# Attention on one core: block turns on VectorE, weighted sums on 32-row array tiles, scores as float32 products on 64-row tiles

## The chip, the cores and the metric

One core of a Trainium2 chip runs the kernel. The metric is device time in microseconds (us) of one execution; profiles give the times of single instructions on the five engines: TensorE (PE for its matmuls, PEld for its weight loads), VectorE (DVE), ScalarE (ACT), GpSimd (POOL) and SyncE (SP, which issues the DMAs).

## The reference

Attention over 8 batches, 8 heads, 576 positions and 64 dimensions, with a learned bias on the scores, and a feed-forward block behind it. All data is float32.

```python
scores = (q @ k.T) / 8                      # per batch and head, 576 x 576
x = log1p(abs(i - j)) / log1p(max(i, 1))    # relative position
bias = relu(x @ w1 + b1) @ w2               # one value per head, i, j
p = exp(scores + bias - rowmax)             # softmax over j
attn = p / (sum(p) + 1e-9)
y = attn @ v                                # -> 4608 tokens x 512
out = ((y @ moe_w1) * (y @ moe_w2)) @ moe_w3 @ moe_w_out
```

## The kernel before

**Stages.** First the bias of all heads is computed and written to DRAM (`nb_d`). Then comes the attention loop. Behind it `moe_w3 @ moe_w_out` is folded into one matrix (`fold`), and then the feed-forward block runs over nine chunks of 512 tokens (`up`, `down`).

**Units.** The loop runs over 32 units: four pairs of heads by eight batches. A unit has nine query tiles of 128 rows: four for each head of the pair (names 0 to 7, even ones of the first head) and a mixed tile M with the last 64 queries of both. In 24 units one piece of the feed-forward weights is also brought from its 64-bit input to float32 in eight small steps (`c0` to `c7`, made by `narrow`): a fetch, two on ScalarE, four on VectorE (clamp L132, shift L135, head L141, power L146) and a last one of two products on GpSimd (L149, L150).

**Steps of a unit.** GpSimd splits q and k into a rounded part and a rest (`op_g`, L250 to L257): the two parts of q stand one above the other on the 128 rows of a tile, k stands twice and its rest twice. `op_S` (L284) then makes a score tile from products of 288 columns over all 128 rows, two per half. `op_T` (L292) is one VectorE instruction that scales, adds the bias and keeps the row minimum of the negated scores; `op_E` (L315) is the exponential on ScalarE with the row sum; `op_r` (L322, L323) the reciprocal of the nine sums. `op_F` (L336 to L349) turns the 128x128 blocks of the exponentials on TensorE by a product with the identity, `op_H` (through `move`, L355 on VectorE and L357 on ScalarE) copies the turned blocks from PSUM to SBUF, and `op_W` (L391) makes the weighted sums from them, the two heads on the two column halves of the array, over 128 keys at a time; `op_X` copies the sums out, `op_x` stores them. The sums are divided later, in the feed-forward stage, by way of the reciprocals in `r_d` (L327, L328).

**Order.** Nothing is ordered by a scheduler: each step has an engine and a time relative to its unit's start in the table `ORDER`, units follow at `PERIOD`, and the steps are issued in the order of these times. An engine runs its instructions in that order and waits where data or a buffer is missing. `NPP`, `NTS` and `NPS` are numbers of buffers for exponentials, score passes and PSUM tiles; scores have two PSUM tiles.

Of the kernel before, what the change touches and what calls it, by code (L numbers as in the profile page):

```python
# [29 lines left out]
PERIOD = 15.82  # L30
ORDER = {
# [4 lines left out]
    },  # L36
    "DVE": {
        "T0": 0.98, "T1": 2.64, "T2": 3.63, "T3": 5.29, "T4": 6.16, "c3": 7.31, "c4": 8.31, "T6": 9.82, "T5": 10.52,
        "c5": 11.22, "c6": 12.22, "T7": 14.31, "H4": 15.01, "TM": 15.82, "HL0": 17.50, "r": 17.84, "HM": 20.14,
        "HN": 22.68,  # L40
    },
    "ACT": {
# [3 lines left out]
    },  # L46
    "POOL": {"gk": -15.50, "gq": -11.40},
    "SP": {"ldk": -30.00, "ldq": -28.00, "ldv": -10.00},
}
TILES = "01234567M"  # L50
NPP, NTS, NPS = 6, 3, 4


def arrange(NU, pieces):

    at = {n: (t, e) for e, steps in ORDER.items() for n, t in steps.items()}
    at["rd"] = at["HN"][0] + 0.8, "SP"
    at["xd"] = max(at["X0"][0], at["X1"][0]) + 0.8, "SP"
    at["c0"] = at["c1"][0] - 4.8, "SP"
    at["c7"] = max(at["c2"][0], at["c6"][0]) + 0.6, "POOL"  # L60
    return {(n, u): (u * PERIOD + t, e) for u in range(NU) for n, (t, e) in at.items() if n[0] != "c" or u in pieces}


@with_exitstack
def relpos_attention_moe(
# [42 lines left out]
    def narrow(pool, src, n, x, queue, pieces=1):  # L108
# [22 lines left out]
        def clamp():  # L131
            nc.vector.tensor_scalar(d["mag"], d["mag"], LEAST, MOST, op0=ALU.max, op1=ALU.min)  # L132
# [60 lines left out]
    st = {u: {"P": [None] * 9} for u in range(NU)}  # L193
# [3 lines left out]

    Q2 = []
    for i in range(2):
        qt = qk.tile([P, 2 * (S + P)], F32R, name=f"Q{i}")  # L200
        nc.gpsimd.memset(f(qt[:, S:S + P]), 0.0)
        Q2.append(qt)

# [7 lines left out]
    def load_bias(p, ts):  # L211
# [9 lines left out]
        if h == 0:  # L221
            nc.sync.dma_start(nb, rows)
        else:
            nc.sync.dma_start(nb[:, :, S - 512:S], rows[:, :, 0:512])
            nc.sync.dma_start(nb[:, :, 0:S - 512], rows[:, :, 512:S])
# [3 lines left out]
    def load(u, which):  # L229
        p, b = units[u]  # L230
        src = {"q": q, "k": k, "v": v}[which]
        if which == "v":
            t = vp.tile([P, v.shape[3]], F32, name="rv", bufs=3)
        else:
            t = raw.tile([P, 2 * S], F32, name=f"r{which}")
        nc.sync.dma_start(t, src[p, b])
        st[u]["r" + which] = t

    def op_ld(u, n):
        load(u, n[1])  # L240

    def op_g(u, n):

        d = st[u]
        x = d.pop("r" + n)
        if n == "q":
            Q = Q2[u % 2]
            Qd = halves(Q)[:, :, 0:S]
# [4 lines left out]
        else:
            K = qk.tile([P, 2 * S], F32R, name="K", bufs=2)
            kl = qk.tile([P, 2 * S], F32R, name="kl", bufs=2)
            nc.gpsimd.tensor_scalar(K, x, 1.0, 1.0, op0=ALU.mult, op1=ALU.mult)
            nc.gpsimd.tensor_tensor(kl, x, f(K), op=ALU.subtract)  # L257
            d.update(K=K, kl=kl)

    def op_S(u, t):  # L260
        d = st[u]
        Q, K, kl = d["Q"], d["K"], d["kl"]
        d["s", t] = ps_s.tile([P, 2, 512], F32, name="s")
        for hf in range(2):
            scores(d["s", t][:, hf, :HS], t, hf, Q, K, kl)

    def scores(s, t, hf, Q, K, kl):
        js = slice(hf * HS, (hf + 1) * HS)
        if t == "M":

            l, m = Q[:, 512:512 + P], Q[:, S + 64:S + 64 + P]
            ops = [(s, l, x[:, js]) for x in (K, kl)]
            if hf == 0:
                ops += [(s, m, x[:, S + 64:S + 64 + HS]) for x in (K, kl)]
            else:
                ops += [(s[:, 0:512 - HS], m, x[:, S + 64 + HS:2 * S]) for x in (K, kl)]
                ops += [(s[:, 512 - HS:HS], m, x[:, S:S + 64]) for x in (K, kl)]
# [509 lines left out]
```

## Time and profile before

| | before |
|---|---|
| median of 3 runs | 1251.35 us (1250.6 to 1251.85) |
| span of the profiled execution | 1248.1 us |
| TensorE matmuls busy | 1210.0 us, 97% |
| VectorE busy | 653.6 us, 52% |
| ScalarE busy | 603.1 us, 48% |
| GpSimd busy | 379.7 us, 30% |
| data moved by DMA | 130.26 MB, 104 GB/s |

The profiled execution is given by its span, from its first to its last instruction; the time of a run also holds what lies around that, and the median of the runs is 3.25 us above the span. In the rows of a profile `x16` is a count, a tile name left of the arrow is written, those right of it are read, `128*64` is the part of the array that is used (rows by columns) and `128x256` the shape of the output. A row in order of time begins with its start and its length in us; a bracket gives the idle time ahead of it and what ended it. A busy matmul is not a matmul at its peak: neighbours overlap, so their starts tell more than their lengths.

### The profile page before, as it was taken

The page shows a single profiled execution, that of the slowest core. Times are in us where ns is not written, and L with a number is a line of the kernel's source. Part 1 is how long each engine was busy: PE and PEld are TensorE (multiplying, and loading weights), DVE is VectorE, ACT ScalarE, POOL GpSimd, SP SyncE. Part 2 cuts the span into 40 slices and gives each one's busy share as a digit, 9 for nine tenths or more (in the row PEclk, how much of TensorE's full clock was granted, in tenths as well). Part 3 has the DMA queues.
Part 4 walks back from the last instruction along what each step waited for, and adds up shares of the span by engine and source line. Part 5 has one row for each costly group of instructions (what it writes and reads, how often), then busy time and mean ns, then how long its engine had stood idle before and what let it go on. Part 6 is the DMA issues. An engine that isn't in the chain of part 4 may idle for free.

```text
span 1248.1 us, 19110 instructions
## 1 busy us (share of the span) xinstructions
PE 1210.0 (97%) x7200; PEld 964.2 (77%) x7200; DVE 653.6 (52%) x1380; ACT 603.1 (48%) x1295; POOL 379.7 (30%) x256
## 2 busy tenths in 40 slices
PE   6789999999999999999999999999999999999998
PEld 1368887777777788887678888888888888888887
DVE  8957776777677767775797522222212231313111
ACT  3768887888788878888444221212121212121211
POOL 5026664666466655661444300000000000000000
PEclk9989999999999999999999999999999999999999
DMA  4874446444644564521543121211111120200000
GB/s 149 285 234 144 142 147 202 142 142 141 222 123 151 151 219 134 145 81 54 133 147 110 60 68 34 68 34 51 51 51 51 42 61 34 68 34 1 20 15 34
DMA packets 60220, 130.26 MB, mean 104 GB/s; under 512 B 8928, under 2 KB 17504, under 8 KB 60128
## 3 DMA queue, kind: packets, MB, share of 16 engines
q1 hardware_dynamic: 59696, 129.02, 33.1%
q8 instruction: 57, 0.93, 0.3%
q14 instruction: 35, 0.29, 0.1%
q10 hardware_dynamic: 432, 0.02, 0.0%
HBM read 99.10 MB, written 29.92 MB: 103 GB/s over the span
## 4 chain that ended last, share of the span: by engine, by line
PE 81%; DVE 10%; DMA 4%; ACT 3%; issue 2%; SPq 0%; ACTq 0%; POOL 0%; DVEq 0%; POOLq 0%
PE up L652 32%; PE o L677 16%; PE pst L391 13%; PE s L284 11%; PE pst L349 5%; DVE r L322 4%; DVE ts L292 3%; PE wacc L611 2%; DMA nb_d<-bev 2%; ACT pt L357 2%; PE bacc L511 1%; DVE zdve L497 1%; DVE px L355 1%; DVE r L323 0%; DMA wi<-in_moe_w_dram 0%
## 5 line engine op out<-in xcount | busy, mean ns | idle before, releaser
L292 DVE CUSTOM_DVE_ANT_0 ts<-s,nb 128x576 f32<-128x576 f32 x256 | 184.6, 748 | 134.7 <-ACT pt L357 73.7
L660 DVE TENSOR_TENSOR g<-up,a 128x512 f32<-128x512 f32 x72 | 49.7, 691 | 343.4 <-PE up L652 343.4
L652 PE MATMUL up<-xh,wl 128*128 128x512 f32 x576 | 225.1, 391 | 0.0
L652 PE MATMUL up<-xl,wh 128*128 128x512 f32 x576 | 225.1, 391 | 0.0
L652 PE MATMUL up<-xh,wh 128*128 128x512 f32 x576 | 225.1, 391 | 0.0
L315 ACT ACTIVATE pp<-ts,mx 128x576 f32<-128x576 f32 x256 | 196.6, 769 | 42.5 <-DVE mx L292 42.5
L284 PE MATMUL s<-K,Q 128*128 128x288 f32 (+2 forms) x672 | 205.6, 325 | 9.2 <-ACT bev L518 3.7
L284 PE MATMUL s<-kl,Q 128*128 128x288 f32 (+2 forms) x672 | 182.3, 295 | 0.0
L677 PE MATMUL o<-w3s,gh 128*128 128x512 f32 x576 | 177.7, 390 | 0.0
L657 ACT COPY a<-up 128x512 f32<-128x512 f32 x72 | 42.2, 587 | 259.6 <-PE up L652 259.6
L638 POOL TENSOR_SCALAR xh<-xr 128x512 fp32r<-128x512 f32 x36 | 23.2, 646 | 445.4 <-DVE xr L634 442.7
L349 PE MATMUL pst<-ident,pp 128*128 128x128 f32 x1024 | 152.4, 277 | 0.2 <-ACT pt L357 0.2
L284 PEld LDWEIGHTS s<-K,Q 128*128 128x128 f32 x672 | 128.0, 191 | 30.1 <-DVE mx L292 13.6
L357 ACT ACTIVATE pt<-pst 128x512 f32<-128x512 f32 x224 | 129.4, 593 | 29.1 <-PE pst L349 24.8
L391 PE MATMUL pst<-pt,rv 128*64 128x320 f32 (+1 forms) x1024 | 138.3, 412 | 1.4 <-DVE pt L355 1.4
L663 ACT ACTIVATE gh<-g 128x512 fp32r<-128x512 f32 x72 | 45.5, 633 | 178.3 <-DVE g L660 178.3
L349 PEld LDWEIGHTS pst<-ident,pp 128*128 128x128 f32 x1024 | 118.5, 141 | 15.7 <-DVE wi L146 11.8
L284 PEld LDWEIGHTS s<-kl,Q 128*128 128x128 f32 x672 | 129.0, 192 | 0.0
L652 PEld LDWEIGHTS up<-xh,wl 128*128 128x128 f32 x576 | 108.2, 188 | 23.4
L652 PEld LDWEIGHTS up<-xl,wh 128*128 128x128 f32 x576 | 108.2, 188 | 23.4
L652 PEld LDWEIGHTS up<-xh,wh 128*128 128x128 f32 x576 | 108.2, 188 | 23.4
L677 PEld LDWEIGHTS o<-w3s,gh 128*128 128x128 f32 x576 | 108.1, 188 | 22.9
(87 smaller groups left out, 1734.2 us busy)
## 6 DMA issues: line engine op xcount, KB each, us to landing
rk<-in_k_dram SPq DMA_DIRECT2D x32, 576.0 KB
rq<-in_q_dram SPq DMA_DIRECT2D x32, 576.0 KB
wi<-in_moe_w_dram SPq DMA_DIRECT2D x32, 512.0 KB
nb_d<-bev SPq DMA_DIRECT2D x36, 295.5 KB
rv<-in_v_dram SPq DMA_DIRECT2D x32, 320.0 KB
x_d<-x SPq DMA_DIRECT2D x32, 288.0 KB
xr<-x_d SPq DMA_DIRECT2D x36, 256.0 KB
rb<-r_d SPq DMA_DIRECT2D x72, 128.0 KB
```

The source lines that it names most:

```text
L284: nc.tensor.matmul(o, l, r, start=(m == 0), stop=(m == len(ops) - 1))
L292: nc.vector.tensor_tensor_reduce(out=halves(ts), in0=d.pop(("s", t))[:, :, :HS], in1=halves(NB[p, t]), op0=ALU.add, op1=ALU.min, scale=-1. ...
L315: nc.scalar.activation(pp, ts, AF.Exp, bias=mx, scale=-1.0, accum_out=d["sum"][:, col:col + 1])
L322: nc.vector.tensor_scalar(r, d["sum"], 1e-9, None, op0=ALU.add)
L349: nc.tensor.transpose(ps[:, c * P:(c + 1) * P], x, ident)
L357: nc.scalar.activation(o, x, AF.Copy)
L391: nc.tensor.matmul(acc[rows], x[:, c0:c0 + D], m, start=(c == 0), stop=(c == 4))
L652: nc.tensor.matmul(acc, l[:, cc], r, start=(n == 0), stop=(n == 3 * NC - 1))
L657: nc.scalar.copy(a, ps[0])
L660: nc.vector.tensor_tensor(g, ps[1], a, op=ALU.mult)
L663: nc.scalar.activation(gh, g, AF.Copy)
L677: nc.tensor.matmul(d["o", t], l[:, sl], folded[ft][:, r], start=(ft == 0 and n == 0), stop=(ft == NF - 1 and n == 2),)
```

## The change

Weighted sums no longer need a full turn. VectorE turns each exponential tile in blocks of 32x32 (`op_R`, into `PT`, SBUF to SBUF), so that a block's 32 keys lie on the 32 rows that its 32 queries had. `op_W` works on 32-row, 64-column tiles of the array: four row groups by two heads, eight tiles, for each of 18 blocks of 32 keys, in four parts (`PARTS`); each row group adds into its own PSUM bank (`acc`, one buffer of four banks). v is loaded four times, once for each row group. TensorE's turns, the copies of the turned blocks and the splitting of q and k on GpSimd go. Scores are plain float32 products on four tiles of 64x64: two halves of the keys on the two row halves, two groups of 64 queries on the two column halves. The reciprocals are turned on VectorE too, and their store takes twelve DMAs in place of two. The clamp of a weight piece moves from VectorE to GpSimd. q, k and v are laid out for this on the host, with no arithmetic. The table of times is replaced by a rule with one slot `L_T` per query tile.

```diff
+L_T = 1.39
+PERIOD = 9 * L_T
 TILES = "01234567M"
-NPP, NTS, NPS = 6, 3, 4
+NPP, NTS = 4, 3
+PARTS = ((0, 5), (5, 9), (9, 14), (14, 18))
+PART_AT = 12, 14, 16, 18
...
+    for k, t in enumerate(TILES):
+        a = k * L_T
+        at["S" + t] = a - 1.1, "PE"
+        at["T" + t] = a + 0.9, "DVE"
+        at["E" + t] = a + 1.7, "ACT"
+        at["R" + t] = a + 2 * L_T + 1.6, "DVE"
+    at["r"] = 10 * L_T + 1.55, "DVE"
+    at["rd"] = 10 * L_T + 2.5, "SP"
+    for n, k in enumerate(PART_AT):
+        at[f"W{n}"] = k * L_T - 0.6, "PE"
+    at["X"] = PART_AT[-1] * L_T + 1.5, "ACT"
+    at["xd"] = at["X"][0] + 0.8, "SP"
+    at["lk"] = -13.0, "SP"
+    at["lq"] = -12.9, "SP"
+    at["lv"] = 1.2 * L_T, "SP"
+    at["c0"] = 0.2, "SP"
+    at["c1"] = 5 * L_T + 2.5, "ACT"
+    at["c2"] = 6 * L_T + 2.5, "ACT"
+    at["c3"] = 6 * L_T + 2.0, "POOL"
+    for n in range(3):
+        at[f"c{4 + n}"] = (7 + n) * L_T + 2.0, "DVE"
+    at["c7"] = 9 * L_T + 3.0, "POOL"
...
-            nc.vector.tensor_scalar(d["mag"], d["mag"], LEAST, MOST, op0=ALU.max, op1=ALU.min)
+            nc.gpsimd.tensor_scalar(d["mag"], d["mag"], LEAST, MOST, op0=ALU.max, op1=ALU.min)
...
+    def op_l(u, which):
...
+            t = vp.tile([P, 2 * NBK * D], F32, name="v4")
+            for a in range(4):
+                nc.sync.dma_start(t[32 * a:32 * a + 32], v[p, b])
...
-    def op_g(u, n):
...
     def op_S(u, t):
+        s = d["s", t] = ps_s.tile([P, 2, 512], F32, name="s")
+        for hf, rows in enumerate((lo, hi)):
+            for g, outs in enumerate((lo, hi)):
...
+                nc.tensor.matmul(
+                    s[outs, hf, :HS], d["q"][rows, h * S + q0:h * S + q0 + 64],
+                    d["k"][rows, h * S + hf * HS:h * S + (hf + 1) * HS], start=True, stop=True,
+                )
...
+    def op_R(u, t):
+        nc.vector.transpose(PT[u % 2][:, SLOT[t]], st[u].pop(("p", t)))
...
+            r = SUMS[u % 3]
+            nc.vector.tensor_scalar(r[:, 0:9], r[:, 0:9], 1e-9, None, op0=ALU.add)
+            nc.vector.reciprocal(r[:, 0:9], r[:, 0:9])
+            d["rt"] = sm.tile([P, 32], F32, name="rt")
+            nc.vector.transpose(d["rt"], r)
...
+        for a in range(4):
+            for h in range(2):
+                o = rows[h, 0:512].rearrange("(i a j) -> a i j", a=4, j=32)[a]
+                nc.sync.dma_start(o, d["rt"][32 * a + 4 * h:32 * a + 4 * h + 4])
+            h, j = a // 2, 512 + a % 2 * 32
+            nc.sync.dma_start(rows[h:h + 1, j:j + 32], d["rt"][32 * a + 8:32 * a + 9])
...
-    def op_F(u, n):
...
-    def op_H(u, n, on):
...
     def op_W(u, n):
+        if n == "0":
+            d["acc"] = ps_t.tile([P, 4, 512], F32, name="acc")
+        acc, pt_, x = d["acc"], PT[u % 2], d["v"]
+        for b in range(*PARTS[int(n)]):
+            for a in range(4):
+                rows = slice(32 * a, 32 * a + 32)
+                for h, outs in enumerate((lo, hi)):
+                    t0, t1 = ((0, 5 if a < 2 else 4), (5 if a < 2 else 4, 9))[h]
+                    c0 = 0 if (h == 1 and a >= 2) else 32
+                    nc.tensor.matmul(
+                        acc[outs, a, c0:c0 + 32 * (t1 - t0)], x[rows, (h * NBK + b) * D:(h * NBK + b + 1) * D],
+                        pt_[rows, t0:t1, 32 * b:32 * b + 32], start=(b == 0), stop=(b == NBK - 1),
+                    )
+    def op_X(u, n):
...
+        nc.scalar.activation(
+            x[:, 0:512].rearrange("p (i a j) -> p a i j", a=4, j=32),
+            acc[:, :, 32:160].rearrange("p a (i j) -> p a i j", j=32), AF.Copy,
+        )
+        for outs, a0, c0 in ((lo, 0, 160), (hi, 2, 0)):
+            nc.scalar.activation(
+                x[outs, 512:S].rearrange("p (a j) -> p a j", j=32), acc[outs, a0:a0 + 2, c0:c0 + 32], AF.Copy,
             )
```

More of the change, by code (lines that the diff above doesn't have):

```diff
@@ L27 @@
 AT_W = 3.5, 0.0, 0.5, 1.2, 2.6, 3.8, 5.5, 7.1, 10.0, 10.6
-PERIOD = 15.82
-ORDER = {
[4 rows of a table removed]
[L36 to L42, printed above, removed]
[3 rows of a table removed]
[L46 to L49, printed above, removed]
+L_T = 1.39
+PERIOD = 9 * L_T
 TILES = "01234567M"
-NPP, NTS, NPS = 6, 3, 4
+NPP, NTS = 4, 3
+PARTS = ((0, 5), (5, 9), (9, 14), (14, 18))
+PART_AT = 12, 14, 16, 18
 def arrange(NU, pieces):
[L56 to L61, printed above, removed]
+    at = {}
+    for k, t in enumerate(TILES):
[20 more added lines that the diff above has]
+    at["c7"] = 9 * L_T + 3.0, "POOL"
+    return {(n, u): (u * PERIOD + t + 1.1, e) for u in range(NU) for n, (t, e) in at.items() if n[0] != "c" or u in pieces}
 @with_exitstack
@@ L192, in relpos_attention_moe @@
     NB = {}
[L193 to L202, printed above, removed]
+    st = {u: {} for u in range(NU)}
     def halves(x):
@@ L220, in load_bias @@
         rows = nb_v[2 * p + h, r0:r0 + 2 * P, :].rearrange("(k p) j -> p k j", p=P)
[L221 to L225, printed above, removed]
+        nc.sync.dma_start(nb, rows)
         for k, t in enumerate(ts):
             NB[p, t] = nb[:, k]
-    def load(u, which):
+    NBK = S // 32
+    def op_l(u, which):
         p, b = units[u]
-        src = {"q": q, "k": k, "v": v}[which]
@@ L260, in op_S @@
+            for a in range(4):
+                nc.sync.dma_start(t[32 * a:32 * a + 32], v[p, b])
+        else:
+            t = raw.tile([P, 2 * S], F32, name=which)
+            nc.sync.dma_start(t, {"q": q, "k": k}[which][p, b])
+        st[u][which] = t
     def op_S(u, t):
         d = st[u]
[L262 to L277, printed above, removed]
-        else:
-            h, i = int(t) % 2, int(t) // 2
-            q0 = h * (S + P + 64) + i * P
-            l = Q[:, q0:q0 + P]
-            ops = [(s, l, x[:, h * S + hf * HS:h * S + (hf + 1) * HS]) for x in (K, kl)]
-        for m, (o, l, r) in enumerate(ops):
-            nc.tensor.matmul(o, l, r, start=(m == 0), stop=(m == len(ops) - 1))
@@ L300, in op_T @@
             load_bias(p + 1, GROUP[t])
+    SUMS = []
+    for i in range(3):
+        t = att.enter_context(tc.tile_pool(name=f"sums{i}", bufs=1)).tile([P, 32], F32, name=f"sums{i}")
+        nc.gpsimd.memset(t, 1.0)
+        SUMS.append(t)
     def op_E(u, t):
@@ L378, in relpos_attention_moe @@
-    QS = (slice(0, 256), slice(256, S))
+            r = SUMS[u % 3]
[3 more added lines that the diff above has]
+            nc.vector.transpose(d["rt"], r)
+            return
+        rows = r_d[p][:, b * S:(b + 1) * S]
+        for a in range(4):
[4 more added lines that the diff above has]
+            nc.sync.dma_start(rows[h:h + 1, j:j + 32], d["rt"][32 * a + 8:32 * a + 9])
@@ L380, in op_W @@
     def op_W(u, n):
         d = st[u]
-        qs, x = QS[int(n)], d["rv"]
-        PT, PX = PTX[u % 2]
-        n_q = qs.stop - qs.start
-        acc = ps_t.tile([P, 512], F32, name="pst")[:, 0:n_q]
-        for c in range(5):
-            for h, rows in enumerate((lo, hi)):
-                c0 = (4 * h + c if c < 4 else 8 + h) * D
-                m = PT[:, c, h * S + qs.start:h * S + qs.stop] if c < 4 else PX[:, qs]
-                nc.tensor.matmul(acc[rows], x[:, c0:c0 + D], m, start=(c == 0), stop=(c == 4))
@@ L537, in relpos_attention_moe @@
     ps_s = att_r.enter_context(tc.tile_pool(name="ps_s", bufs=2, space=PSUM, side="right"))
-    ps_t = att.enter_context(tc.tile_pool(name="ps_t", bufs=NPS, space=PSUM))
-    PTX = [(pt.tile([P, 4, 2 * S], F32, name=f"pt{i}"), pt.tile([P, S], F32, name=f"px{i}")) for i in range(2)]
+    ps_t = att.enter_context(tc.tile_pool(name="ps_t", bufs=1, space=PSUM))
+    PT = [pt.tile([P, 9, S], F32, name=f"pt{i}") for i in range(2)]
     drive([e for e in later if e[0] < t_s])
```

121 lines of the change are left out of this document (16 added, 105 removed), and 7 rows, old and new, of the table ORDER.

## The prediction

> **What bounds the kernel now.** I read the page's busy line first, then busy time by stage, then the groups, then the order of time on TensorE and on VectorE.
>
> ```profile
> span 1248.1 us, 19110 instructions
> PE 1210.0 (97%) x7200; PEld 964.2 (77%) x7200; DVE 653.6 (52%) x1380; ACT 603.1 (48%) x1295; POOL 379.7 (30%) x256
> 88.25:585.56 497.31, 493.15 (x3876) 398.42 (x3875) 365.05 (x901) 397.55 (x916) 287.94 (x167) 1.00 0.47 146
> 88.43 1.78 DVE L322 TENSOR_SCALAR r<-sum 128x9 f32<-128x9 f32 x1
> 585.71 0.17 DVE L322 TENSOR_SCALAR r<-sum 128x9 f32<-128x9 f32 x1 [0.66 <-ACT ppM L315]
> ```
>
> The third row covers the attention loop (columns: length, then busy time of PE, PEld, DVE, ACT, POOL, granted clock, DMA share, GB/s). TensorE is busy for 493 of 497 us at full clock; VectorE for 365, ScalarE for 398. TensorE sets the pace. Line 322 runs once per unit, so its first and its last row, 31 units apart, give the period: (585.71 - 88.43)/31 = 16.04 us. 32 such units are 513 us; the expert stage behind them is not touched by the change. So the question is which engine bounds a unit afterwards, and at how many us.
>
> **TensorE after the change.** All its turns (line 349 and its neighbours, with the copies behind them on ScalarE and VectorE) go. What comes are float32 products on small tiles of the array: 36 for the scores and 144 for the weighted sums in a unit. Whether small tiles work side by side decides everything, so I look for that in rows:
>
> ```profile
> 301.18 0.29 PE L284 MATMUL s<-kl,Q 128*128 128x288 f32 x1
> 301.40 1.95 PE L391 MATMUL pst<-pt,rv 128*64 128x256 f32 x16
> 303.18 0.60 PE L391 MATMUL pst<-px,rv 128*64 128x256 f32 x4
> 303.71 0.40 PE L284 MATMUL s<-K,Q 128*128 128x288 f32 x1
> 303.95 0.29 PE L284 MATMUL s<-kl,Q 128*128 128x288 f32 x1
> 304.08 0.29 PE L284 MATMUL s<-K,Q 128*128 128x288 f32 x1
> ...
> 305.40 2.37 PE L391 MATMUL pst<-pt,rv 128*64 128x320 f32 x16
> 307.60 0.71 PE L391 MATMUL pst<-px,rv 128*64 128x320 f32 x4
> ...
> 64.57 0.62 PE L511 MATMUL bacc<-zact,w2b 128*32 128x512 f32 x1 [0.35 <-ACT zact L495]
> 64.57 0.78 PE L511 MATMUL bacc<-zdve,w2b 128*32 128x512 f32 x7
> 65.45 0.18 PE L511 MATMUL bacc<-zact,w2b 128*32 128x16 f32 x1
> ```
>
> A weighted sum is 5 x 2 products in the code and 20 instructions in the trace, so a float32 product is two instructions. Sixteen of 256 columns start over 1.78 us, 0.111 each, and sixteen of 320 over 2.20 us, 0.138 each. In the prologue, four tiles of 32 columns with 512 moving columns (8 instructions) are through in 0.88 us, 0.110 each. The simplest reading of both: a tile streams at 0.85 ns a column, so 512 columns cost 0.44 us, and four tiles overlap fully; 256 columns cost 0.22, and the pair overlaps fully. Column tiles, then, work side by side, four deep. That tiles of different rows do so too, no row shows.
>
> I take it that they do. Scores: two instructions per tile at 288 x 0.85 = 0.245, 0.49 us for a tile of 128 queries, 0.54 with its first weight load; nine make 4.9. Weighted sums: 18 blocks x 2 instructions, each round of eight tiles as long as its widest, 160 columns, 0.136 us: 4.9 us. Changing from scores to sums costs about 0.1 to 0.2 us (last score at 301.18, sums at 301.40, where 0.13 is the score's own; back again 0.10 and a first score that takes 0.24 instead of 0.13); four parts are eight changes, 1.2 us. TensorE needs 11.0 us a unit where it now has 16.04. From the other end: if rows do not overlap at all, the scores double (8.7) and the sums are four times as long (19.6), 29.5 us with the changes.
>
> **VectorE after the change.** It keeps the nine score passes (line 292), gets nine turns of 128x576, keeps the small reciprocals with a turn of 128x32 behind them, and loses the copies of line 355 and the clamp, which goes to GpSimd.
>
> ```profile
> 305.18 0.76 DVE L292 CUSTOM_DVE_ANT_0 ts<-s,nb 128x576 f32<-128x576 f32 x1 [1.30 <-PE s L284]
> 305.86 0.08 DVE L292 DVE_READ_ACCUMULATOR2_ANT mx<- 128x1 f32 x1
> 305.86 0.75 DVE L292 CUSTOM_DVE_ANT_0 ts<-s,nb 128x576 f32<-128x576 f32 x1
> ...
> 306.54 0.69 DVE L141 SCALAR_TENSOR_TENSOR wmag<-wi,wmag 128x512 int32<-128x512 int32 x1
> 307.26 0.43 DVE L146 TENSOR_SCALAR wi<-wmag 128x512 int32<-128x512 int32 x1
> ...
> 312.88 0.42 DVE L355 COPY px<-pst 128x256 f32<-128x256 f32 x1
> 313.22 1.72 DVE L322 TENSOR_SCALAR r<-sum 128x9 f32<-128x9 f32 x1
> 314.97 0.22 DVE L323 RECIPROCAL r<-r 128x9 f32<-128x9 f32 x1
> 316.40 0.69 DVE L355 COPY pt<-pst 128x512 f32<-128x512 f32 x1
> 317.00 0.75 DVE L292 CUSTOM_DVE_ANT_0 ts<-s,nb 128x576 f32<-128x576 f32 x1
> ```
>
> A score pass holds VectorE for 0.68 us (start to start), its accumulator read included; nine are 6.12. A copy of 512 columns holds it 0.60, one of 256 0.34: 1.02 ns a column. No row shows a turn. Below it lies the form of line 146 (0.43 for 512 columns, so about 0.41 held for 576), above it twice the column rate, 1.27. It is nearest to the score pass in columns and type, so 0.68, and I add 0.03 because a 32-column block has to be in before it can come out: 0.71, nine are 6.39. The Trainium skill (VectorE: DVE Perf Modes, The three transpose paths) gives 311 ns for a 128-column bf16 turn; my estimate from it for 576 columns is a duration near 0.78, held about 0.71 us, with which the sum would not change. No run here shows it.
>
> The reciprocal group: 0.17 (the row at 585.71), about 0.30 for the reciprocal until a dependent instruction can go, 0.12 for the small turn: 0.60. Plain unit: 6.12 + 6.39 + 0.60 = 13.11 us.
>
> 24 of the 32 units also convert a piece of weights: shift, head and power (lines 135, 141, 146), 0.43 + 0.69 + 0.43 less 0.08 of overlap each, 1.31 us. And they meet a wait:
>
> ```profile
> 307.92 1.27 POOL L149 TENSOR_TENSOR w3s<-w3s,wi 128x512 f32<-128x512 f32 x1 [5.17 <-DVE wi L146]
> 309.27 1.29 POOL L150 TENSOR_TENSOR w3s<-wmag,w3s 128x512 f32<-128x512 f32 x1
> 312.24 2.66 POOL L257 TENSOR_TENSOR kl<-rk,K 128x1152 fp32r<-128x1152 f32 x1
> ```
>
> Line 322 takes 0.17 us while GpSimd rests (585.71) and 1.72 at 313.22, where it ends at 314.94, just behind GpSimd's 312.24 + 2.66 = 314.90: it waits until GpSimd's instruction is over. The long GpSimd passes on q and k go with the change, but its two products behind the last piece step (lines 149 and 150) stay: the first starts 307.92 - 307.26 = 0.66 us after that step's start. In the new order that step is followed on VectorE by a score pass of the next unit and then by the reciprocal group. The step holds VectorE 0.35, the score pass 0.68, so the group is reached at 1.03 and is let through at 0.66 + 1.27 = 1.93: 0.90 us of stall, between nothing (GpSimd late) and 2.2 (both products ahead). Queued behind it on VectorE are the unit's last turn, for which the first weighted sum waits, and the next score pass. Piece unit: 13.11 + 1.31 + 0.90 = 15.32. Mean: (24 x 15.32 + 8 x 13.11)/32 = 14.77 us. VectorE becomes the bound, 92% of today's period.
>
> **What lies beside it.** ScalarE: nine exponentials, the two piece steps it has now, and the copy out of the sums in three instructions; SP: the issues of the DMAs:
>
> ```profile
> 306.00 0.77 ACT L315 ACTIVATE pp<-ts,mx 128x576 f32<-128x576 f32 x1
> 306.76 0.76 ACT L315 ACTIVATE pp<-ts,mx 128x576 f32<-128x576 f32 x1
> 305.51 0.60 ACT L357 ACTIVATE pt<-pst 128x512 f32<-128x512 f32 x1
> 303.19 0.61 SPq L327 DMA_DIRECT2D r_d<-rt  x1
> 302.77 0.33 SPq L236 DMA_DIRECT2D rq<-in_q_dram  x1
> DMA packets 738, 2.37 MB, mean 148 GB/s; under 512 B 86, under 2 KB 94, under 8 KB 735
> GB/s 138 287 379 368 138 87 0 20 0 195 92 368 345 368 92 23 0 0 0 0 0 0 0 0 0 102 153 153 102 225 235 311 388 403 411 287 110 0 0 126
> ```
>
> ScalarE: 9 x 0.76 + about 1.0 for the copy + 1.3 for the steps = 9.1 us, hidden. GpSimd: a clamp (estimate 0.6) and the two products, 3.2 us, hidden but for the stall above. SP's queue: two issues of the reciprocals become twelve, one of v becomes four: 12 x 0.61 + 6 x 0.33 + two others of about 0.4 is 10.1 us of issuing in 14.77, and behind the twelve stand the next unit's q and k, planned 5.8 slots of the nine later (8 us): hidden, with little to spare. Data: v goes from 320 to 4 x 288 KB, so 2.37 MB becomes 3.20 MB a unit (the last two rows are one period of 16.04 us), 217 GB/s, where the chip moves up to 411 in a slice: hidden.
>
> One cover is thin. A score tile may start when the score pass two before it has ended; VectorE then has 2.1 us of other work (turn, pass, turn). In four of nine slots TensorE puts a part of the sums in between: five blocks of 2 x 0.136 are 1.36, with changes and the score itself 2.2 us, made up in the slot after. If that slips by 0.3 us in each, the unit costs 1.2 us more. I take nothing, and keep 0.3 of it for the upper end.
>
> **The sum.** 32 x (16.04 - 14.77) = 41 us gained; the fold stage behind the loop has the same TensorE work, less about as much turning as the new parts add, so nothing there. Span 1248.1 - 41 = 1207; the median of the runs, 1251.35, stands 3.25 above the profiled span: 1211. Own range of this case: turns held 0.65, no stall and a group of 0.45 give 1.35 us a unit less, 1168; turns at 0.77 and slipping parts 0.84 more, 1238. The far ends of the turn are rivals.
>
> **Rivals.**
> TensorE stays the bound because row tiles overlap only by halves. The rounds then take 0.27: 9.8 + 4.9 + 1.2 = 15.9 us and its waits on VectorE on top, 16.0 to 17.6: 1250 to 1301. It decides from about 0.27 us a round; at 0.136 TensorE has a quarter of the period free. For it: no row shows rows side by side. Against it: column tiles overlap fully.
> No overlap of rows: 29.5 us, 32 x 13.5 = 431 us more, 1682.
> Turns at twice the column time (1.27): VectorE 14.77 + 9 x 0.56 = 19.8 us, 1372. At 0.41 VectorE needs 12.1 us and comes near TensorE's 11.0: 1125.
> TensorE cannot issue so many small instructions: 360 products a unit, 24 a us, where the loop has issued 3876 in 497 us, 8 a us, and a 64-column product has followed its neighbour in 0.04 us:
>
> ```profile
> 310.71 0.20 PE L284 MATMUL s<-K,Q 128*128 128x64 f32 x1
> 310.75 0.28 PE L284 MATMUL s<-kl,Q 128*128 128x64 f32 x1
> ...
> 64.59 0.11 PEld L511 LDWEIGHTS bacc<-zact,w2b 128*32 128x32 f32 x1
> 64.60 0.20 PEld L511 LDWEIGHTS bacc<-zdve,w2b 128*32 128x32 f32 x4
> ```
>
> At 0.04 each, a round of eight takes 0.32: 11.5 + 4.9 + 1.2 = 17.6 us, 1301; at 0.06 each, 0.48: 17.3 + 4.9 + 1.2 = 23.4 us, 1487. It decides from 0.034, where a round is 0.27. Against it: four weight loads on four tiles, 0.11 each, are over 0.20 after the first began, 0.03 apart, a product behind each; but that is a burst, and nothing in this trace lasts. The Trainium skill (TensorE: Matmul & The Clock Gate, Wait — 56ns, not 53.3ns?) speaks for this rival: with hardware decode off, the sequencer spends about 62 ns on each matmul; by that, as an estimate, 360 take 22.3 us a unit and the time would be 1452. The same page (Part 3, Measured speedup vs the span model) gives 3.07 times the speed for four row tiles, which speaks for the forecast. No run here shows either.
>
> **How the numbers follow.** VectorE as the bound with row tiles side by side: 0.62. Half overlap of rows: 0.08. Issue at 0.04 or slower: 0.08. No row overlap: 0.07. Turns at double time: 0.08. Below 1168, cheaper turns: 0.07. Forecast 1211. Range 1150 to 1301: it leaves out no overlap, double turns and half of the issue case (0.19), and little below. All of the first case is faster, as is the last; of the half-overlap case I give 0.01 to faster and 0.03 to within 0.2%, about what a measurement of this kernel can tell from no change: faster 0.70, within 0.2% 0.03, slower 0.27.
>
> **What would show it.** A period near 14.8 us between the small adds ahead of the reciprocal, 15.3 in piece units and 13.1 in others; VectorE over 95% busy in the loop; turns starting 0.7 us before their successor; those small adds at 1 us or more in piece units and 0.2 in the rest; sum products of one round starting together with rounds 0.136 apart. Wrong, if TensorE shows no idle time in the loop: then rounds are longer than 0.27, and their spacing says whether rows or issue are at fault; or if turns take over 1 us.

## The result, and the profile after

The changed kernel takes 1338.69 us (median of 4 runs, 1334.24 to 1344.74), beside 1250.97 for the kernel before: a ratio of 1.0709, 95% interval 1.0679 to 1.0738. It is slower by 88 us where 40 us of gain were forecast, and it lies outside the range (1150 to 1301).

The first lines of the profile after, then the attention loop from 82 to 620 us for after and for before (columns: length, busy time of PE, PEld, DVE, ACT, POOL, granted clock, DMA share, GB/s), then the small add ahead of the reciprocal, one in each unit (shortest, median and longest length in ns; first and last start):

```profile
span 1342.9 us, 34477 instructions
PE 1147.8 (85%) x14720; PEld 825.3 (61%) x14720; DVE 709.0 (53%) x1468; ACT 495.2 (37%) x1071; POOL 213.8 (16%) x169
82.00:620.00 538.00, 394.00 (x10085) 240.49 (x10084) 402.66 (x910) 266.61 (x637) 97.99 (x66) 0.85 0.63 177
...
L288 DVE TENSOR_SCALAR sums<-sums x32: 166/841/853, 76.9 to 664.3; 128x9 f32<-128x9 f32 x32
```

```profile
82.00:620.00 538.00, 529.71 (x4086) 427.18 (x4085) 392.33 (x951) 423.55 (x968) 303.22 (x178) 1.00 0.48 147
```

Before, TensorE is busy for 530 of 538 us. After, nothing is full: TensorE 394, VectorE 403, ScalarE 267. No engine bounds the loop, so it is waiting that does. From the first to the last of the small adds pass 587.4 us (497.3 before; the forecast's 31 x 14.77 is 457.9). From the last one to the end pass 678.7 us (662.4 before). The first comes at 76.9 (88.4 before). So 90.1 us are lost in the loop, 16.3 behind it, and 11.5 are won ahead of it. The next two readings are those two losses.

**The loop.** TensorE's rows in order of time, and VectorE's at the same place:

```profile
286.00 1.62 PE L313 MATMUL acc<-pt,v 32*64 32x160 f32 x80 [0.69 <-ACT pp L275]
287.55 1.20 PE L243 MATMUL s<-k,q 64*64 64x288 f32 x16
288.68 0.80 PE L313 MATMUL acc<-pt,v 32*64 32x160 f32 x32
293.38 1.03 PE L313 MATMUL acc<-pt,v 32*64 32x160 f32 x29 [3.90 <-issue]
```

```profile
295.85 0.76 DVE L254 CUSTOM_DVE_ANT_0 ts<-s,nb 128x576 f32<-128x576 f32 x1 [4.56 <-PE s L243]
```

In the middle of one part of the sums TensorE stands still for 3.90 us. The bracket says "issue": it waits for nothing that a semaphore would show. VectorE is out of score tiles soon after and loses 4.56 us. Over the whole run the list of waits has 97.9 us in 45 places under `PE acc L313 <- issue`, most of it such stops. What ends such a stop is seen in the DMA queues. Here are the queue rows of the page, after and then before, and those of two stretches of after, 285.0 to 290.2 and 290.2 to 291.6 us:

```profile
q8 instruction: 115, 1.88, 0.6%
```

```profile
q8 instruction: 57, 0.93, 0.3%
```

```profile
DMA packets 240, 1.19 MB, mean 228 GB/s; under 512 B 40, under 2 KB 40, under 8 KB 168
q1 hardware_dynamic: 240, 1.19, 87.3%
...
DMA packets 47, 0.29 MB, mean 209 GB/s; under 512 B 16, under 2 KB 16, under 8 KB 16
q1 hardware_dynamic: 46, 0.28, 87.6%
q8 instruction: 1, 0.02, 5.7%
```

Queue 8 moves instructions, in pieces of 16 KB. TensorE's matmuls and weight loads (2 x 14720 after, 2 x 7200 before), divided by 115 and 57 pieces, are 256 and 253 to a piece. From 285.0 to 290.2 us the DMA engines are busy with data for 87% of the time: a 512 KB weight piece, issued at 284.60, and then v, whose four loads were issued from 285.03 on. For these five microseconds no instruction piece moves; one starts at 290.39 and lands at 291.65, and TensorE goes on at 293.38.

From the packets of queue 8 and TensorE's records I worked out, for each piece, when it is due and whether TensorE runs out. In the kernel before, a fetch starts (median 0.21 us after this point) when some 263 instructions are left ahead; I call that point due. "Empty" is a gap of over 0.7 us between the last instruction of the reserve and the first of the new piece. Before, 31 fetches in the loop: at most 1.25 us late, none empty, as 263 instructions last about 16 us. After, 85 fetches: median 4.48 us late, up to 7.97, about 1.1 us of transfer, some 1.3 to 1.7 us more until TensorE runs; 29 empty stretches, 95.8 us in all. Ahead of these 29 the reserve lasted 4.5 us (median; 3.4 to 6.5): 80 instructions of the sums and their 80 weight loads pass in 1.55 us (286.00 to 287.55), and scores and short waits lie between such bursts. The loop is 90 us longer.

Two more counts of the same records tie the stops to the pieces and to the data. Counted along TensorE's records (weight loads, matmuls and its sequencer's), the 29 stretches all lie a whole multiple of 256 apart, while TensorE's other stops fall on other places of a piece each time. And while the fetches ahead of these 29 were late, 33.7 MB of data moved: 24.0 of v, 4.6 of weight pieces and 2.8 of q and k, told apart by the size of their packets; v was among it every time.

**Behind the loop.** The fold stage, in order of time on GpSimd, VectorE and TensorE, and two rows of the chains of waits over the whole run:

```profile
680.41 1.92 POOL L134 TENSOR_SCALAR wmag<-wmag 128x512 f32<-128x512 f32 x1
...
682.36 0.43 DVE L137 TENSOR_SCALAR wmag<-wmag 128x512 int32<-128x512 int32 x1 [4.41 <-POOL wmag L134]
682.70 0.68 DVE L542 TENSOR_TENSOR w3s<-wacc,w3s 128x512 fp32r<-128x512 f32 x1
683.30 0.68 DVE L528 TENSOR_TENSOR w3l<-w3t,w3h 128x512 fp32r<-128x512 f32 x1
...
684.04 1.12 PE L522 MATMUL w3t<-ident,w3s 128*128 128x128 f32 x4 [4.12 <-DVE w3l L528]
...
DVE wmag L137 <- POOL wmag L134: 34.3, 26, 4.4
PE w3t L522 <- DVE w3l L528: 10.7, 8, 4.1
```

The clamp in the kernel before, on VectorE (shortest, median and longest length in ns):

```profile
L132 DVE TENSOR_SCALAR wmag<-wmag x40: 403/405/1518, 94.3 to 697.9; 128x512 f32<-128x512 f32 x40
```

It took 0.41 us there and takes 1.92 us on GpSimd (L134). `narrow`, in which it was moved, also converts the 16 pieces of weights of this stage. VectorE's shift (L137) waits 4.41 us for it, the fold's subtraction (L528) is queued behind the shift, and TensorE stands 4.12 us.

**What did come as forecast.** VectorE while it had work:

```profile
306.18 0.77 DVE L281 STREAM_TRANSPOSE pt<-pp 128x576 f32<-128x576 f32 x1
306.88 0.72 DVE L254 CUSTOM_DVE_ANT_0 ts<-s,nb 128x576 f32<-128x576 f32 x1
307.53 0.08 DVE L254 DVE_READ_ACCUMULATOR2_ANT mx<- 128x1 f32 x1
307.53 0.77 DVE L281 STREAM_TRANSPOSE pt<-pp 128x576 f32<-128x576 f32 x1
```

A turn holds it for 0.70 us (306.18 to 306.88), a score pass with its read for 0.65.

### The profile page after: what moved, and what is told of

It reads as the page before. It is cut to its first block, busy times and chain, and to the rows that moved or that the text cites. A ratio compares the mean times of both kernels' runs of the same rounds, so it can differ in the third digit from the quotient of the medians.

```text
span 1342.9 us, 34477 instructions
## 1 busy us (share of the span) xinstructions
PE 1147.8 (85%) x14720; PEld 825.3 (61%) x14720; DVE 709.0 (53%) x1468; ACT 495.2 (37%) x1071; POOL 213.8 (16%) x169
## 3 DMA queue, kind: packets, MB, share of 16 engines
q1 hardware_dynamic: 60912, 156.30, 39.6%
## 5 line engine op out<-in xcount | busy, mean ns | idle before, releaser
L313 PE MATMUL acc<-pt,v 32*64 32x160 f32 (+1 forms) x9216 | 247.7, 338 | 109.1 <-issue 97.9
L275 ACT ACTIVATE pp<-ts,mx 128x576 f32<-128x576 f32 x288 | 223.1, 775 | 289.5 <-DVE mx L254 285.3
L313 PEld LDWEIGHTS acc<-pt,v 32*64 32x64 f32 x9216 | 195.9, 154 | 184.1 <-issue 166.6
L243 PE MATMUL s<-k,q 64*64 64x288 f32 x2304 | 217.4, 480 | 56.4 <-DVE mx L254 39.0
L281 DVE STREAM_TRANSPOSE pt<-pp 128x576 f32<-128x576 f32 x288 | 221.5, 769 | 0.3 <-ACT pp L275 0.3
L243 PEld LDWEIGHTS s<-k,q 64*64 64x64 f32 x2304 | 78.2, 150 | 156.9 <-DVE mx L254 85.3
L134 POOL TENSOR_SCALAR wmag<-wmag 128x512 f32<-128x512 f32 x40 | 78.7, 1969 | 355.5 <-ACT wmag L128 354.9
L600 PE MATMUL o<-w3s,gl 128*128 128x512 f32 x288 | 112.3, 390 | 0.9 <-DVE gl L589 0.9
L589 DVE TENSOR_TENSOR gl<-g,gh 128x512 fp32r<-128x512 f32 x72 | 50.8, 705 | 51.5 <-ACT gh L586 51.5
```

Source lines behind the costliest of these rows:

```text
L134: nc.gpsimd.tensor_scalar(d["mag"], d["mag"], LEAST, MOST, op0=ALU.max, op1=ALU.min)
L243: nc.tensor.matmul(s[outs, hf, :HS], d["q"][rows, h * S + q0:h * S + q0 + 64], d["k"][rows, h * S + hf * HS:h * S + (hf + 1) * HS], start= ...
L275: nc.scalar.activation(pp, ts, AF.Exp, bias=mx, scale=-1.0, accum_out=SUMS[u % 3][:, col:col + 1])
L281: nc.vector.transpose(PT[u % 2][:, SLOT[t]], st[u].pop(("p", t)))
L313: nc.tensor.matmul(acc[outs, a, c0:c0 + 32 * (t1 - t0)], x[rows, (h * NBK + b) * D:(h * NBK + b + 1) * D], pt_[rows, t0:t1, 32 * b:32 * b ...
L589: nc.vector.tensor_tensor(gl, g, f(gh), op=ALU.subtract)
```

## The experiments

All ran beside the kernel before, whose medians were 1250.0 to 1252.2 in these comparisons. "Late" is the median start of an instruction fetch after it was due, "empty" the count and sum of the empty stretches (both in the loop, worked out as above), "loop" and "tail" the times from the first small add to the last and from there to the end; these four are from the profiled execution.

| kernel | median us | ratio to before, 95% interval | late | empty | loop | tail |
|---|---|---|---|---|---|---|
| before | 1250.97 | 1 | 0.21 | 0 | 497.3 | 662.4 |
| after | 1338.69 | 1.0709 (1.0679 to 1.0738) | 4.48 | 29, 95.8 | 587.4 | 678.7 |
| e1 v once | 1271.23 | 1.0179 (1.0121 to 1.0238) | 2.13 | 11, 21.1 | 514.9 | 678.8 |
| e2 v apart | 1288.69 | 1.0290 (1.0256 to 1.0324) | 2.79 | 14, 17.6 | 530.6 | 679.3 |
| e3 eight parts | 1289.27 | 1.0295 (1.0248 to 1.0341) | 3.14 | 28, 59.3 | 532.1 | 680.8 |
| e4 both | 1265.07 | 1.0109 (1.0064 to 1.0154) | 2.42 | 12, 15.4 | 504.2 | 681.0 |
| e5 before, v three times | 1252.82 | 1.0009 (0.9995 to 1.0023) | 0.28 | 0 | 502.9 | 661.3 |
| e6 half the products | 1265.69 | 1.0126 (1.0100 to 1.0153) | 3.98 | 7, 6.8 | 503.2 | 683.8 |
| e7 clamp on VectorE | 1320.32 | 1.0562 (1.0533 to 1.0591) | 4.05 | 30, 85.0 | 579.6 | 662.4 |
| e8 = e4 + e7 | 1253.15 | 1.0020 (0.9997 to 1.0042) | 2.45 | 14, 19.9 | 512.7 | 665.0 |
| e9 = e8, stores by GpSimd | 1305.65 | 1.0437 (1.0417 to 1.0457) | 3.91 | 35, 83.2 | 559.6 | 667.6 |
| e10 = e8, v once, copied | 1281.95 | 1.0243 (1.0190 to 1.0296) | 1.63 | 6, 9.9 | 529.2 | 664.3 |
| e11 = e9 + e10, q apart | 1317.22 | 1.0547 (1.0514 to 1.0580) | 1.61 | 7, 8.1 | 561.3 | 670.2 |
| e12 = e8, sums a slot later | 1252.11 | 1.0025 (0.9994 to 1.0057) | 2.94 | 22, 35.2 | 507.2 | 664.2 |
| e13 = e12, q apart | 1251.40 | 1.0012 (0.9996 to 1.0028) | 2.73 | 22, 37.5 | 510.3 | 665.5 |
| e14 = e8, half the products | 1243.99 | 0.9957 (0.9933 to 0.9980) | 1.89 | 1, 1.4 | 497.8 | 663.6 |
| e15 = e12, stores later | 1242.24 | 0.9922 (0.9903 to 0.9941) | 2.62 | 21, 36.3 | 498.2 | 665.0 |
| e16 = e8, stores later | 1261.76 | 1.0108 (1.0057 to 1.0159) | 2.88 | 27, 53.1 | 518.2 | 662.5 |

### e1 to e4: less data, data apart, sums apart

The theory was that instruction pieces wait behind v's data while the sums use instructions in bursts; the rivals, that the bursts alone do it, or that TensorE waits for other engines' work.

e1, v in one load of 288 KB a unit after the first two units (`V4` are two fixed buffers; three of the four row groups keep the v of the first two units, so this kernel leaves out most of v):

```diff
-            t = vp.tile([P, 2 * NBK * D], F32, name="v4")
-            for a in range(4):
+            t = V4[u % 2]
+            for a in range(4 if u < 2 else 1):
...
```

> The changed kernel, but v is brought by one DMA of 288 KB per unit instead of four (after the first two units the other three row groups keep the v of those units, so the sums of later units are made from old data there). Theory 1: TensorE's instructions come in pieces of 16 KB, and the request for the next piece stands about 5 us behind v's 1.15 MB, so TensorE runs dry once in a unit for 3 to 4 us. Then the requests start within 2 us, the dry stretches of over 2 us go, the period falls from 19.3 to 15 or 15.5 us and the time to 1210 to 1245. Rival 2: TensorE uses up its instructions in the parts of the sums faster than any fetch brings them, whatever else moves: one dry stretch a unit stays, 1310 or more. Rival 3: the waits between VectorE and TensorE around the two score tiles make the gaps: no change, 1330 to 1345.

e2, the four loads two slots apart:

```diff
-    at["lv"] = 1.2 * L_T, "SP"
+    for a in range(4):
+        at[f"lv{a}"] = (1.2 + 2 * a) * L_T, "SP"
...
```

> The changed kernel with v's four DMAs issued two slots apart instead of in a row, same bytes. Theory 1: a request then stands behind 288 KB at most, about 1.2 us, and other loads; dry stretches shrink to under 1.5 us, period 15.5 to 17, time 1225 to 1275. Rival 2 and rival 3: no change, 1330 to 1345.

e3, the sums in eight parts, one in each slot:

```diff
-PARTS = ((0, 5), (5, 9), (9, 14), (14, 18))
-PART_AT = 12, 14, 16, 18
+PARTS = ((0, 3), (3, 5), (5, 7), (7, 9), (9, 12), (12, 14), (14, 16), (16, 18))
+PART_AT = 12, 13, 14, 15, 16, 17, 18, 19
```

> The changed kernel with the sums in eight parts of two or three blocks in eight slots, instead of four parts of four or five in every second slot; v as it was. Theory 1: the request still waits about 5 us and lands 7.5 us after it was due, while the last 260 instructions now last about 4.5 us instead of 3: a stretch of 2 to 3 us stays, 1290 to 1325. Rival 2: the bursts are gone, and with them the dry stretches, 1215 to 1250. Rival 3: more changes between tile shapes and more score tiles behind a part, 1340 to 1400.

e4 is e2 and e3 together.

> Both: eight parts, and v's four DMAs two slots apart. Theory 1: the last 260 instructions last about 4.5 us and a fetch needs about 4, so TensorE hardly runs dry: VectorE is the bound, period 15 to 15.5, time 1210 to 1240. Rival 2: the same as with eight parts alone. Rival 3: 1340 to 1400.

With TensorE's instructions unchanged, e1 takes 67 us off the time, and fetches are half as late. The same data in four loads apart (e2) take 50 off, the same data with smaller bursts (e3) 49, both together (e4) 74. So lateness and bursts each cost, and either cure removes over half: bursts alone are not it. The rival of waits for other engines, which expected no gain, is out. But the theory's ranges were missed too: e1, e2 and e4 came out 26, 14 and 25 us above theirs, and e3 just under its own. In e4 the loop is within 7 us of before, while the tail stays 16 to 19 us longer than before in all four: a second cause, and part of the 14 to 26 us.

### e5 and e6: the data without the instructions, half the instructions with the data

e5, in the kernel before:

```diff
+            for i in range(2):
+                nc.sync.dma_start(vp.tile([P, v.shape[3]], F32, name=f"rx{i}", bufs=1), src[p, b])
```

> The kernel before, with v loaded three times in each unit, the two added copies (2 x 320 KB) into tiles that nothing reads: its loads grow to what the changed kernel asks for. Theory (TensorE's instructions come in pieces of 256 over a queue that shares the DMA engines with the data; before, a reserve lasts about 15 us, so a fetch that is late by some microseconds costs nothing): same time, 1251 +- 3 us, with fetches that start 2 to 5 us late in place of 0.2 and no empty stretch. Rival (the added data slow the kernel by themselves, by what they take from the DMA engines or from memory): the loop's period grows, by 1 us a unit or more, 1285 us or above.

e6, in the changed kernel, with the sums over every second block of 32 keys (half of the keys are left out of them):

```diff
-        for b in range(*PARTS[int(n)]):
+        for b in range(PARTS[int(n)][0] + PARTS[int(n)][0] % 2, PARTS[int(n)][1], 2):
...
```

> The changed kernel with the sums over every second block of 32 keys only (72 products a unit in place of 144, so the output is not attention over all keys); all loads, turns and waits stay, v's four loads too. Theory (instruction supply): 216 records a unit in place of 360, so that a reserve of about 263 outlasts a fetch that starts 4.5 us late; few empty stretches are left, and the period falls from 19.3 to VectorE's 14.5 to 16 us: 1190 to 1240 us. Rival (TensorE waits for work of other engines, turns or scores): only the sums' own time goes, 2.4 us of 4.9 a unit, and what of it was hidden stays: 1262 to 1330 us. Rival (the data of v's loads slow all): as that, near 1330.

e5 is as fast as before with as much data, 187 GB/s from 100 to 580 us against after's 178: the volume by itself costs nothing. The other half of its expectation failed: its fetches were not 2 to 5 us late but 0.28 (3.41 at most). So it doesn't show that a late fetch is harmless with a long reserve, and lateness doesn't follow from volume alone; what queues ahead at that moment counts. e6 shows the reserve's part: all of after's loads, fetches still 3.98 us late, and only 7 empty stretches of 6.8 us in place of 29 of 95.8. Its time, 73 us less, is none the less above the 1190 to 1240 expected, and it lies in the range of the rival by which only the sums' own time goes (1262 to 1330). So the time does not tell the two apart; the stretches do, and what TensorE and VectorE wait for in their place. The loop's busy time, 100 to 580 us, and two chains of waits in the same stretch:

```profile
100.00:580.00 480.00, 343.31 (x6333) 161.92 (x6316) 421.27 (x949) 278.31 (x660) 102.38 (x69) 0.78 0.72 201
...
PE s L243 <- DVE mx L254: 103.2, 110, 5.8
...
DVE wmag L137 <- POOL wmag L134: 22.7, 19, 5.5
```

TensorE now waits for VectorE (25.8 us in after), but VectorE is at 421 of 480 us: it waits for the clamp on GpSimd, 22.7 us in this stretch, 2.0 in after, where TensorE's stops covered that wait.

### e7 and e8: the clamp

```diff
-            nc.gpsimd.tensor_scalar(d["mag"], d["mag"], LEAST, MOST, op0=ALU.max, op1=ALU.min)
+            nc.vector.tensor_scalar(d["mag"], d["mag"], LEAST, MOST, op0=ALU.max, op1=ALU.min)
```

> The changed kernel with the clamp of the weights' halves back on VectorE, where it was before; all else as changed. Theory (the clamp on GpSimd takes 1.92 us for each piece where VectorE took 0.40, and in the stage after the loop VectorE's shift waits for it, with the fold's subtraction queued behind): the stage from the last unit's reciprocal to the end goes from 679 back to 662 us; in the loop the 0.67 us stall of the add behind GpSimd goes, and TensorE's empty stretches hide most of what that gives: 1322 us, 1312 to 1327. Rival (the later stage is longer because it starts with a slower clock or with other loads): no change there, 1335 to 1345.

e8 is e4 with this edit.

> The kernel with v's four loads apart and the sums in eight parts, with the clamp on VectorE besides. If the two causes add up: 1265 - 17 = 1248 us in the later stage alone; the loop, where VectorE is 88% busy, gains up to 0.3 us a unit by the stall that goes or loses as much by the clamp's 0.4: 1238 to 1256, about the time before. If the later stage's length has another cause: 1262 to 1268.

e7 takes 18 us off, and the tail is 662.4 us, as before: this second cause is settled. The small add's stall isn't: it still takes 0.84 us in e7's piece units, so it stands behind GpSimd's products and not behind the clamp. e8 adds both cures: 1253 us, no different from before. The forecast's mechanism, VectorE as the bound, would have given 1211. So 40 us were still open. In e8 VectorE is busy for 419 of 480 us, and what it waits for is:

```profile
DVE ts L257 <- PE s L246: 46.6, 42, 4.8
DVE ts L257 <- DMA nb<-nb_d: 8.7, 2, 4.8
```

### e9 to e11: taking load off the queues by way of GpSimd

e9 issues the twelve stores of the reciprocals on GpSimd (`nc.gpsimd.dma_start` in place of `nc.sync.dma_start`).

> The kernel with both cures (v's loads apart, sums in eight parts, clamp on VectorE) with the twelve small stores of the reciprocals issued by GpSimd in place of SyncE, so that a load of v is not queued behind them. Theory (at a change of pair the sums wait for v's pieces, which SyncE issues late): TensorE's waits on v go, some 5 of 8 such places, 3 us each: 1238 us, 1230 to 1248. Rival (instruction supply alone holds what is left, some 20 us of empty stretches): same as before the edit, 1249 to 1257.

e10 loads v once and copies it:

```diff
+            if a == 0:
+                nc.sync.dma_start(t[0:32], v[p, b])
+            else:
+                nc.gpsimd.tensor_copy(t[32 * a:32 * a + 32], t[0:32])
...
```

> The kernel with both cures, with v loaded once a unit (288 KB into partitions 0 to 31) and put into the other three row blocks by GpSimd copies; the whole computation is done. Theory (what keeps the instruction pieces waiting is the data of the other loads): 0.86 MB a unit less, fetches start under 2 us late, at most 5 empty stretches; the period falls from 16.7 towards VectorE's 14.5: 1190 to 1225 us. Rival (GpSimd's copies slow VectorE, or are themselves late for the sums): period 16 or more, 1245 us and up, with VectorE's turns or score passes longer than 0.70 and 0.67 us, or TensorE waiting for the copies.

e11 has both, and q's load later.

> As the run with v loaded once and copied by GpSimd, with the small stores on GpSimd's queue and q's load 3.9 us after k's. Theory (loads in bursts hold fetches up): a little less than that run, by 0 to 15 us: 1185 to 1220. Rival (GpSimd's order: copies queued behind stores that wait for the reciprocals): 5 to 30 us more than that run.

All three are worse than e8, and e9 and e11 lie outside what their theory and their rival expected. In e10 the instruction theory held in its own numbers (fetches 1.63 us late, 6 empty stretches of 9.9 us), and its rival, that GpSimd's copies slow VectorE, fits the time, though by other passes than it named: VectorE is busy for 436 of 480 us at 17.1 us a unit, 15.5 us of work, where e8 has 419 of 480 at 16.5, 14.4 us. VectorE's clamp and shift in e8 (L135, L138), the same two in e10 (L136, L139), and e10's copy, all from 100 to 580 us:

```profile
L135 DVE TENSOR_SCALAR wmag<-wmag 128x512 f32<-128x512 f32 x23 | 8.9, 385 | 0.0
L138 DVE TENSOR_SCALAR wmag<-wmag 128x512 int32<-128x512 int32 x23 | 8.8, 384 | 0.0
```

```profile
L139 DVE TENSOR_SCALAR wmag<-wmag 128x512 int32<-128x512 int32 x22 | 21.0, 956 | 0.0
L136 DVE TENSOR_SCALAR wmag<-wmag 128x512 f32<-128x512 f32 x22 | 20.5, 931 | 0.0
L234 POOL COPY v<-v 32x2304 f32<-32x2304 f32 x84 | 179.5, 2137 | 167.4 <-DMA v<-in_v_dram 137.8 <-PE s L251 15.3 <-DMA r_d<-rt 10.9
```

GpSimd's copies take 2.14 us each, and VectorE's clamp and shift go from 0.385 to 0.93 and 0.96 us, the head (L145) from 0.65 to 0.82. Turns and score passes keep their lengths (0.768 and 0.736 in e10). The Trainium skill (SBUF — State Buffer, 🔬 SBUF: two separate sides) states it as an exclusive lock on a port pair that VectorE's two-port passes and GpSimd share, held for a whole instruction; the small add of 0.84 us and these rows agree.

In e9 the stores, 0.53 us each on GpSimd, travel in 12288 packets of their own queue, where before the edit they were 2304 of queue 1 (60912 less 58608):

```profile
q1 hardware_dynamic: 58608, 156.15, 41.9%
q8 instruction: 115, 1.88, 0.7%
q0 software_dynamic: 12288, 0.18, 0.7%
```

Fetches are later again (3.91 us) and the empty stretches are back at 83.2 us. Whether it is these packets that hold them up was not tried by itself; in e11, where the same 12288 packets travel and v is loaded once, fetches are 1.61 us late and 8.1 us are empty, so the packets alone don't do it.

### e12 to e16: the order of what is left

e12 puts the sums one slot and v's loads two slots later (`PART_AT = 13, ... 20`, `(3.2 + 2 * a) * L_T`).

> The kernel with both cures, with all eight parts of the sums and v's loads put one slot (1.39 us) and two slots later. Theory (what is left of VectorE's idle time, 57 of 480 us, comes from TensorE's order: the first part waits 1.7 us for the unit's last turn and the score tiles behind it come late): that wait falls under 0.7 us, the period goes from 16.7 to 15.5 to 16, 1215 to 1240 us. Rival (instruction pieces that come late hold it): the empty stretches stay, near 14 and 20 us, 1247 to 1258.

e13 has q's load 3.9 us behind k's besides (`at["lq"] = -9.0`).

> As the run with the parts one slot later, with q's load 3.9 us after k's. Theory (two loads of 576 KB at once hold up the instruction pieces): fetches start at a median of 2 us late or less, fewer than 10 empty stretches, 3 to 15 us less than that run. Rival (fetches are delayed by the mean load, not by this burst): within 3 us of that run.

e14 is e8 with e6's halving.

> The kernel with both cures, with the sums over every second block of keys (the output is not attention over all keys). Theory (with few instructions TensorE neither runs dry nor stands in VectorE's way): VectorE over 95% busy, period 14.5 to 15.2, 1195 to 1215 us, which is then what the changed kernel could reach at most by its VectorE work. Rival (VectorE waits for loads of the bias or for ScalarE's exponentials): period near 16, 1235 us or above.

e15 is e12, and e16 is e8, with the reciprocals' stores later:

```diff
-    at["rd"] = 10 * L_T + 2.5, "SP"
+    at["rd"] = 19 * L_T, "SP"
```

(17 in e16.)

> The kernel with both cures and the sums one slot later, with the reciprocals' twelve small stores moved behind v's last load in SyncE's order. Theory (at a change of pair SyncE spent 187 to 200 us of the profile on these stores while v's second load stood behind them, and VectorE lost 9.2, 8.7 and 7.6 us there for want of scores): the three stops fall under 4 us each, the period goes from 16.5 to 15.8 or less, 1225 to 1240 us, below the time before. Rival (v's loads come late there because the DMA engines are full with the bias loads): stops of 6 us and more stay, 1247 to 1257 us.

> The kernel with both cures (sums at the earlier slots) with the reciprocals' twelve small stores moved behind v's last load. Theory (stores in front of v): the stops of 4 to 5 us at the changes of pair go, 1235 to 1248 us. Rival (full DMA engines): as without the move, 1247 to 1258 us.

e12 and e13 moved nothing. The wait of the sums for a unit's last turn, 23.8 us from 100 to 580 us in e8, is gone in e12; what that gave was lost again as 8 more empty stretches and in stops at the changes of pair. TensorE's row at one of them, and SyncE's rows:

```profile
199.01 1.86 PE L316 MATMUL acc<-pt,v 32*64 32x128 f32 x36 [7.99 <-DMA v<-in_v_dram]
```

```profile
184.97 1.00 SPq L211 DMA_DIRECT2D nbM<-nb_d  x1
186.07 0.54 SPq L233 DMA_DIRECT2D k<-in_k_dram  x1
186.66 0.73 SPq L233 DMA_DIRECT2D q<-in_q_dram  x1
187.44 1.57 SPq L229 DMA_DIRECT2D v<-in_v_dram  x1
189.26 1.50 SPq L300 DMA_DIRECT2D r_d<-rt  x2
192.87 0.21 SPq L302 DMA_DIRECT2D r_d<-rt  x1
...
198.11 1.12 SPq L300 DMA_DIRECT2D r_d<-rt  x2
...
200.54 0.32 SPq L229 DMA_DIRECT2D v<-in_v_dram  x1
```

TensorE waits 7.99 us for v. The theory laid this on the stores of half a kilobyte, behind which the next piece of v is issued only at 200.54. But TensorE goes on at 199.01, so the piece it waited for is the one issued at 187.44, the last of this unit and ahead of the stores; the one at 200.54 is the next unit's. From 190 to 194 us the data queue moves packets of 2304 and 4608 bytes, the sizes of bias rows and of k and q, and none of v's 9216. So at this stop the other loads stood ahead of v, as e15's rival has it, and not the stores. Moving the stores made e15 the kernel with the lowest time of the study, 1242.24 us, 0.8% less than before, but not by the step expected: three stops of 6.1, 7.7 and 8.2 us stay (on VectorE, from 194, 321 and 453 us), as its rival had it: at the first of them TensorE goes on at 197.20, with a piece of v that was issued at 185.87, again ahead of the stores. By which step the move helped stays open. The same move in e16 made the time longer, with 27 empty stretches. A load that shifts by a slot meets other fetches, and which of them come out empty isn't foreseen by any of the theories.

e14 is the plainest: with one empty stretch left, VectorE is 91% busy:

```profile
100.00:580.00 480.00, 369.09 (x6434) 145.06 (x6431) 435.13 (x981) 286.67 (x674) 60.85 (x48) 0.81 0.72 205
```

It takes 1244 us, so the expected 95% and 1195 to 1215 were not reached even so. This falls to its rival's side (1235 us or above). VectorE waits for score tiles 64 times in this stretch, 34 us. TensorE for its part waits 35.9 us for a unit's last turn, in 25 places, with score tiles behind it in its order; whether a later slot for the sums, as in e12, would free them here was not tried, so the cause of these last waits stays open.

## Why the prediction was wrong, point by point

- **TensorE's work, row tiles side by side: right.** Eighty instructions of the sums, ten rounds of eight, pass in 1.55 us (286.00 to 287.55), 0.155 a round with the change of shape, where 0.136 was taken, 0.27 for half overlap. A score tile takes 0.57 us (16 instructions for two of them, 287.55 to 288.68) for 0.54.
- **The rival of issue: wrong in its rate.** It put TensorE's limit at the rate of issue, 0.04 us or more for each instruction (its 360 products a unit are instructions, two to a product). The row shows 0.019 (1.55/80). The Trainium skill (TensorE: Matmul & The Clock Gate, Wait — 56ns, not 53.3ns?) has 62 ns for a matmul without hardware decode; here the measurement is less than a third of that, and no run shows which way instructions are decoded. It was right to be wary of the number of instructions, but what limits is their supply, which no part of the text priced.
- **"Hidden", said of the data: the step that failed.** The rise to 3.2 MB a unit was set against what the engines can move, as if bandwidth were all. It was not the volume that cost (e5): v's four loads in one burst, with a weight piece ahead of them in most units, kept the next 16 KB of instructions waiting, and the change had also cut the reserve from about 16 us to 4.5 where it ran out. That is 95.8 us of empty stretches; e1 and e6 remove most of them, from either side. The profile before had what was needed: the instruction queue's own row, 57 pieces for 14400 records.
- **VectorE's work: right.** Turn 0.70 (0.71), score pass 0.65 to 0.68 (0.68). The stall of the small add is there, 0.84 less 0.17 = 0.67 us in piece units (0.90 was taken). Sum: 402.66 of 538 us, and a unit takes 587.4/31 = 18.95 us on the mean, so 14.2 us of VectorE a unit against 14.77. That is 75% of the time, where over 95% was to show it as the bound: TensorE's stops reach it as missing score tiles.
- **"So nothing there", said of the fold stage, and the clamp at 0.6 us: wrong.** The clamp takes 1.92 us, and the shared `narrow` puts it in the fold stage's path, where it costs 16.3 us of tail (678.7 less 662.4 in e7). The step looked only at the instructions that the loop issues.
- **The thin cover at score tiles** was kept for the upper end only. Waits of VectorE for score tiles are what is left when the two causes are cured (VectorE at 87% in e8, 91% in e14); how much of that is the slip that the text meant was not shown.
- **In numbers:** forecast loop 31 x 14.77 = 457.9, measured 587.4: 129.5 us more, of which 95.8 are empty stretches. The other 33.7 were not taken apart; e14, nearly free of such stretches, still has a loop 39.9 us above the forecast. Tail 16.3 more, head 11.5 less (not foreseen, and its cause was not found). 1207.4 + 129.5 + 16.3 - 11.5 is 1341.7, and the last unit's 1.3, which the forecast had also taken off, makes 1343.0, the span within rounding.

## What to carry to other kernels

When a change trades few large products for many small ones, count the instructions and price their supply: how long does the reserve last at the new rate, and which loads can stand ahead of the next piece when it is due. Spread such loads and such bursts before looking for more bandwidth; e4 needed no less data than after and won 74 us. When a step moves to another engine, follow every caller of the function it is in, and read the new engine's duration from a row of the same form.

## What the runs showed of the hardware that was not expected

- TensorE's instructions come during the run in pieces of 16 KB, 256 instructions, over the engines that move data. In the kernel before, a fetch starts when about 263 instructions are left; it takes about 1.1 us when it moves, and after an empty stretch TensorE runs 1.3 to 1.7 us after it lands. At a median of 4.48 us of waiting ahead of it, 29 of 85 fetches of the changed kernel came too late.
- A clamp of 128x512 (maximum and minimum) takes 1.92 us on GpSimd and 0.39 to 0.41 on VectorE; GpSimd's product of two tiles of that shape takes 1.27.
- The reciprocals' small stores (128 and 512 bytes), issued by GpSimd, went in 12288 packets, 5.3 times as many as from SyncE, and cost GpSimd 0.53 us each.
